# A written-out order of single operations, all stores by SyncE, a first chunk in halves and fewer warming products in a gated-linear-attention and mixture-of-attention kernel

## The chip, the cores and the metric

The kernel runs on one core of one Trainium2 chip. The metric is the device time of one execution in microseconds (us), as the median of several runs; smaller is better. Every time below is in us unless ns is written. The engines are PE (TensorE), DVE (VectorE), ACT (ScalarE), POOL (GpSimd) and SP (SyncE, which only issues transfers).

## The reference, cut to what matters

```python
for t in range(S):                       # B, H, S, D = 4, 8, 768, 48
    state = alpha[t, :, None] * state + outer(k[t], v[t])
    y[t] = q[t] @ state
x = y as (B, S, 384)
logits = x @ w_gate                      # 4 experts, the best 2 weighted by a softmax
for e in range(4):                       # Hd = 64
    q, k, v = x @ wq[e], x @ wk[e], x @ wv[e]
    a = softmax(causal(q @ k.T / 8))
    out += weight[e] * (a @ v @ wo[e])
```

## The kernel before, in words

**Stage one** turns the recurrence into 24 chunks of 128 tokens, six for each of the four batches. For chunk n, DVE makes the running products of alpha by two scans (L466 backwards, L489 forwards) and scales k (L493) and q (L497). PE then makes the products of k and q (`pa`, L527), transposes k (`pt`, L554), updates the state (`pu`, L572, for which ACT first copies the transposed k, `kt`), and makes the chunk's output (`py`, L618) from the masked products `ms`. The mask of one half is put on by DVE (L536), that of the other by an ACT copy (L539) and a POOL selection (L543).

**Stage two** works in eight units u of three chunks (384 tokens): projections of q and k (`pj`, L660; for unit 0 in plain fp32, L890, straight from the loaded weights `wqk`), values and gate (`pv`, L687; L679 for unit 0), scores (`sc`, L749), their masked copy with a running maximum on DVE (L758), the exponential on ACT (L767), the weighting on POOL (L786), transpositions (`tr`, L804) with a copy on ACT (L818), the product with the values (`yv`, L841), its split in two parts on ACT and DVE (L850, L852), and the output projection (`po`, L867), copied by ACT (L873) and stored. SP issues all loads and the stores (L879), save the last two stores, which ACT issues itself (L876).

**Form of a product.** PE uses its array in several forms: whole (`pj`, `pv`, `po`; transpositions `tr`, `pt`), in two bands of rows (`pa`, `sc`), in two bands of columns (`pu`, `yv`) or in four (`py`). All products write to eight PSUM banks `g`.

**What sets the order.** Every operation is recorded with the operations that it has to follow, its engine and the buffers that it uses. A planner with costs of its own for each operation then walks through them, and at each step takes, engine by engine, the ready operation of the lowest rank. The rank comes from `TURN`, a table of 552 numbers that orders groups of operations. Each engine's instructions are written down in the resulting order and run strictly in it. Before the first use of the last bank, the planner fills every gap that it expects on PE with products of zeros (`warm`, L1095), whose operand `zb` lies in the constant `d1r`.

**Verdict.** ACT squares and sums the running products of each chunk (L509). At the end a number made from these sums (`verdict`: two DVE instructions L514 and L515, a product on PE at L517, a DVE copy at L519) is read by every engine (L1104), which then branches round a slow exact version.

Of the kernel before, what the change touches and what calls it, by code (L numbers as in the profile page):

```python
# [49 lines left out]
STICK = 100  # L50
DMA_FIXED = 1.5
DMA_RATE = 250.0
LOOK = 0.05
WARM_GAP = 0.45
WARM_MM = 0.11
GB = 8
HINT = {"PE": 9.0, "V": 120.0, "A": 120.0, "G": 60.0, "S": 200.0}
TURN = (
# [24 lines left out]
)  # L83
# [1123 lines left out]
```

## Time and profile before

| | |
|---|---|
| time, median of 3 runs | 317.26 us (316.0 to 317.34) |
| profiled execution: own time, span of its instructions | 317.55 us, 315.8 us |
| PE, DVE, ACT, POOL busy in the span | 307.5, 243.9, 228.7, 119.1 us |
| products on PE, of these warming products | 3809, 56 |
| loaded, stored | 25.39 MB, 4.72 MB |

The own time is 1.75 us longer than the span, which runs from the first instruction to the last. A product in plain fp32 that isn't a transposition is recorded twice. Busy time of PE is the time in which any product is in flight: products overlap, so that the step from one start to the next tells more than the length of one.

### The profile page before, as it was taken

What the parts mean: (1) busy time and instruction counts of PE and PEld (TensorE: products, weight loads), DVE (VectorE), ACT (ScalarE), POOL (GpSimd) and SP (SyncE); (2) the same over time, 40 slices, a digit from 0 to 9 for tenths busy, and PEclk for the clock granted to TensorE, in tenths of its full rate; (3) what the DMA queues carried; (4) which work ended last, traced back from release to release, by engine and by line L of the source; (5) the groups of instructions that cost most, each with busy time, mean ns of one, the idle gap of its engine ahead of it and who ended that gap; (6) DMA issues with size and microseconds to landing.
All of it is one profiled execution on the core that took longest, in us unless ns stands there. A gap on an engine that the chain in (4) does not pass through costs nothing.

```text
span 315.8 us, 9736 instructions
## 1 busy us (share of the span) xinstructions
PE 307.5 (97%) x3809; PEld 270.4 (86%) x3809; DVE 243.9 (77%) x708; ACT 228.7 (72%) x591; POOL 119.1 (38%) x174
## 2 busy tenths in 40 slices
PE   8999999999999999999999999999999999999991
PEld 5899988999897998798999799899889978988791
DVE  6889999989899998898899999853883555376530
ACT  0885797576897799876696979965677886759661
POOL 5221464202651356561172646350507060507130
PEclk9999999999999999999999999999999999999998
DMA  7999933535513254331721440300101000012001
GB/s 205 296 241 228 234 124 124 169 88 155 153 26 117 72 155 124 103 103 55 220 98 28 115 134 16 112 4 1 52 27 51 28 2 1 2 50 75 27 29 56
DMA packets 14195, 30.79 MB, mean 97 GB/s; under 512 B 1664, under 2 KB 4960, under 8 KB 14144
## 3 DMA queue, kind: packets, MB, share of 16 engines
q1 hardware_dynamic: 13856, 29.72, 32.9%
q8 instruction: 31, 0.51, 0.7%
q10 hardware_dynamic: 288, 0.39, 0.3%
q14 instruction: 20, 0.16, 0.2%
HBM read 25.39 MB, written 4.72 MB: 95 GB/s over the span
## 4 chain that ended last, share of the span: by engine, by line
PE 94%; DVE 2%; ACT 1%; ACTq 1%; issue 1%; POOL 0%; POOLq 0%
PE g L660 14%; PE g L804 12%; PE g L841 12%; PE g L618 11%; PE g L749 10%; PE g L867 8%; PE g L527 7%; PE g L687 7%; PE g L572 3%; PE g L1095 3%; PE g L554 2%; PE g L890 2%; PE g L679 1%; ACTq L876 1%; DVE al L466 0%
## 5 line engine op out<-in xcount | busy, mean ns | idle before, releaser
L786 POOL TENSOR_SCALAR a<-a,cf,gw 128x128 f32<-128x128 f32 (+5 forms) x96 | 80.7, 854 | 77.0 <-DVE cf L779 19.6
L767 ACT ACTIVATE a<-a,mx 128x128 f32<-128x128 f32 (+5 forms) x96 | 63.3, 661 | 12.2 <-DVE mx L758 11.6
L758 DVE CUSTOM_DVE_ANT_0 a<-g,cm 128x384 f32<-128x384 f32 (+3 forms) x96 | 46.9, 529 | 9.6 <-PE g L749 9.4
L818 ACT ACTIVATE at<-g 128x512 f32<-128x512 f32 (+3 forms) x124 | 48.9, 465 | 1.2 <-PE g L804 0.6
L804 PE MATMUL g<-ident,a 128*128 128x128 f32 x336 | 46.1, 276 | 0.1
L804 PEld LDWEIGHTS g<-ident,a 128*128 128x128 f32 x336 | 37.9, 141 | 4.0 <-POOL a L786 1.2
L841 PE MATMUL g<-at,vg 128*64 128x384 f32 (+2 forms) x324 | 39.4, 391 | 0.0
L749 PE MATMUL g<-k,q 64*128 64x256 f32 (+3 forms) x384 | 37.6, 331 | 0.0
L841 PEld LDWEIGHTS g<-at,vg 128*64 128x64 f32 x324 | 21.7, 137 | 16.9 <-issue 13.6
L749 PEld LDWEIGHTS g<-k,q 64*128 64x128 f32 x384 | 29.8, 185 | 4.1 <-issue 0.6
L618 PE MATMUL g<-ms,vt 128*32 128x128 f32 x768 | 33.2, 275 | 0.0
L543 POOL TENSOR_SCALAR_AFFINE_SELECT ms<-ms 128x512 f32<-128x512 f32 x24 | 17.3, 722 | 41.8 <-ACT ms L539 41.7
L466 DVE TENSOR_TENSOR_SCAN al<-al,d1r 112x516 f32<-112x516 f32 (+1 forms) x25 | 30.5, 1226 | 1.6 <-POOL mask L432 1.6
L489 DVE TENSOR_TENSOR_SCAN al<-al,d1c 112x516 f32<-112x516 f32 (+1 forms) x25 | 30.5, 1223 | 0.2
L660 PE MATMUL g<-xh,wqk_h 128*128 128x384 f32 x84 | 29.8, 355 | 0.0
L660 PE MATMUL g<-xh,wqk_l 128*128 128x384 f32 x84 | 28.3, 337 | 0.0
L660 PE MATMUL g<-xl,wqk_h 128*128 128x384 f32 x84 | 28.2, 336 | 0.0
L509 ACT ACTIVATE al<-al 112x1033 f32<-112x1033 f32 x24 | 25.6, 1066 | 2.5 <-issue 1.6
L527 PE MATMUL g<-qk 48*128 48x128 f32 x384 | 26.1, 279 | 0.0
L527 PEld LDWEIGHTS g<-qk 48*128 48x128 f32 x384 | 23.2, 187 | 1.9 <-issue 0.6
L618 PE MATMUL g<-qk,S 112*32 112x128 f32 x480 | 24.2, 272 | 0.0
L589 POOL TENSOR_TENSOR C<-C,ev 112x192 f32<-112x192 f32 x16 | 10.4, 652 | 35.2 <-DVE C L587 30.6
(100 smaller groups left out, 642.3 us busy)
## 6 DMA issues: line engine op xcount, KB each, us to landing
qk<-in_qk_dram SPq DMA_DIRECT2D x24, 448.0 KB, 4.4
vt<-in_v_dram SPq DMA_DIRECT2D x25, 256.0 KB, 4.4
al<-in_al_dram SPq DMA_DIRECT2D x24, 226.2 KB, 4.1
out_dram<-ot SPq DMA_DIRECT2D x22, 192.0 KB, 1.9
at<-in_wqk_dram SPq DMA_DIRECT2D x1, 768.0 KB, 9.6
qk<-in_qk_dram SPq DMA_DIRECT2D x2, 224.0 KB, 3.4
at<-in_wvg_dram SPq DMA_DIRECT2D x1, 390.0 KB, 7.8
at<-in_wo_dram SPq DMA_DIRECT2D x1, 384.0 KB, 10.8
```

What stands on the lines that cost most here:

```text
L466: V.tensor_tensor_scan(backwards(al[0:P, AW + c0 - 1:AW + c1 - 1]), backwards(al[0:P, c0:c1]), d1r[0:P, sl].rearrange("p a w -> p (a w)"), ...
L489: V.tensor_tensor_scan(c, c, T(("d1c", n))[0:P, sl].rearrange("p a w -> p (a w)"), 0.0, OP.mult, OP.max)
L527: PE.matmul(T(("pa", n, s))[:, C * p:C * p + C], t[r:r + D, p, C:2 * C], t[r:r + D, p, 0:C], start=True, stop=True, tile_position=(r, 0))
L618: PE.matmul(py[32 * j:32 * j + 32, k], l, r, start=(i == 0), stop=(i == len(parts) - 1), tile_position=(0, 32 * j))
L660: PE.matmul(pj[:, :W3], w[:, kt, cs], x[:, kt, :], start=(i == 0), stop=(i == 8))
L749: PE.matmul(T(sk[e])[:, :w], q[r, x, ts], k[r, y, c0:c1], start=(m == 0), stop=(m == 2), tile_position=(64 * e, 0))
L758: V.tensor_tensor_reduce(T(ak[e])[:, c0:c1], T(sk[e])[:, :w], cm[:, m0:m0 + w], -1.0, mx[:, 0:1] if x else BIG, OP.add, OP.min, accum_out= ...
L767: A.activation(a[:, 0:n], a[:, 0:n], AF.Exp, bias=T(mk)[:, e, len(pieces) - 1:len(pieces)], scale=-1.0, accum_out=T(("sm", u))[:, ix:ix + 1])
L786: G.tensor_scalar(a[:, 0:n], a[:, 0:n], T(ck_)[:, e:e + 1], T(("gw", u))[:, i, eg:eg + 1], op0=OP.mult, op1=OP.mult)
L804: PE.transpose(pt[:, 128 * (j - j0):128 * (j - j0) + 128], a[:, 128 * j:128 * j + 128], ident)
L818: A.activation(dst, src, AF.Copy)
L841: PE.matmul(py[64 * e:64 * e + 64, lo:n1], v[:, j % 3, 64 * eg:64 * eg + 64], at[e][:, at_off(j) + lo:at_off(j) + n1], start=(j == 0), sto ...
```

## The change

1. `TURN` and the planner's choice among ready operations go. `ORDER` lists all 1573 operations one by one, and the planner only works out buffers and start times along it. Its costs are finer: a price for each pair of forms of a product, and slower products in the first 6 us.
2. Every store is issued by SP.
3. In chunk 0, `pt`, `pa`, the mask and `py` work on halves of two head pairs each, and DVE masks both parts.
4. A first exponential on a tile `junk` is added on ACT.
5. The warming products read a tile of their own (`zb` in an output buffer), and their number follows the new start times: 33 in place of 56.
6. Weights wait in planned `at` buffers, and not in fixed ones.

```diff
-TURN = (
-    215, 75, 5, 3, 42, 289, 74, 30, 19, 90, 221, 119, ...
+ORDER = (
+    15, 7, 0, 2, 4, 1, 3, 8, 6, 21, 31, 22, 24, 23, 13, 32, ...
...
-    def schedule(self, timed=True, turn=()):
+    def schedule(self, order=None):
...
+        for i in order:
             o = ops[i]
+            e = o["eng"]
+            assert (o["preds"] | o["claims"]) <= done
+            t = at[e]
+            for j in o["preds"]:
+                q = ops[j]
+                if q["eng"] != e or q["dma"]:
+                    t = max(t, q["end"] + SEM)
...
             if o["pe"]:
-                t = max(rt[i], t + change(o))
+                t = max(t, at["PE"] + turnover(state, o["pe"]))
+                state = o["pe"]
...
-                    warm(int(gap / WARM_MM * 0.8))
+                    cold = max(0.0, min(gap, COLD - pe))
+                    warm(int((cold / WARM_MM[0] + (gap - cold) / WARM_MM[1]) * 0.85))
...
-    zb = d1r.rearrange("p a b -> p (a b)").bitcast(BF)[:, 0:256]
+    zb = pools["ot"][1][:, 0:128].bitcast(BF)
...
+            op("G", 0.1, 0.15, lambda T: (G.memset(zb, 0.0), G.memset(junk, 0.0)) and None, w=whole(("junk",), ("zb",)), port=False)
+            op("A", 1.4, 1.5, lambda T: A.activation(junk, junk, AF.Exp), w=whole(("junk",)))
...
-                if s == 0 and n >= MS_ACT:
-                    op("V", 0.61, 0.69, f0, r=whole(("pa", n, s), ("mask",)), w=[(("ms", n), s)])
+                if n == 0 or (s == 0 and n >= MS_ACT):
+                    o, l = vec(np * C)
+                    op("V", o, l, f0, r=rd + whole(("mask",)), w=wr)
...
-            if u == NU - 1 and i:
-                op("A", 0.36, 0, lambda T: A.dma_start(out_d[b, t0:t0 + 128, :], T(("ot", u, i))),
-                   r=whole(("ot", u, i)), dma=196608)
-            else:
-                op("S", 0.06, 0, lambda T: SY.dma_start(out_d[b, t0:t0 + 128, :], T(("ot", u, i))),
-                   r=whole(("ot", u, i)), dma=196608)
+            op("S", 0.43, 0, lambda T: SY.dma_start(out_d[b, t0:t0 + 128, :], T(("ot", u, i))),
+               r=whole(("ot", u, i)), dma=196608)
...
                 for p in (0, 2):
                     prep_r(0, p, 2)
                     prep_c(0, p, 2)
+                    gla_t(0, p, 2)
+                    gla_a(0, p, 2)
```

DVE at the start of the program, before: chunk 0 (buffers `al_71`, `qk_75`) is prepared whole, then chunk 1's scans (`al_72`) follow, and the mask of chunk 0 (L536).

```order
L466 SCALAR_TENSOR_TENSOR al_71<-al_71,d1r 112x258 x2
L470 RECIPROCAL d1c_87<-al_71 112x2
L493 TENSOR_TENSOR qk_75<-qk_75,al_71 112x2x128
L470 RECIPROCAL d1c_87<-al_71 112x2
L489 SCALAR_TENSOR_TENSOR al_71<-al_71,d1c_87 112x258 x2
L497 TENSOR_TENSOR qk_75<-qk_75,al_71 112x2x128
L493 TENSOR_TENSOR qk_75<-qk_75,al_71 112x2x128
L497 TENSOR_TENSOR qk_75<-qk_75,al_71 112x2x128
L466 SCALAR_TENSOR_TENSOR al_72<-al_72,d1r 112x516
L470 RECIPROCAL d1c_87<-al_72 112x4
L489 SCALAR_TENSOR_TENSOR al_72<-al_72,d1c_87 112x516
L536 TENSOR_TENSOR ms_90<-g_64,mask 128x512
```

And now (the mask is L541 here):

```order
L493 TENSOR_TENSOR qk_75<-qk_75,al_71 112x2x128
L489 SCALAR_TENSOR_TENSOR al_71<-al_71,d1c_87 112x258
L470 RECIPROCAL d1c_87<-al_71 112x2
L493 TENSOR_TENSOR qk_75<-qk_75,al_71 112x2x128
L497 TENSOR_TENSOR qk_75<-qk_75,al_71 112x2x128
L466 SCALAR_TENSOR_TENSOR al_72<-al_72,d1r 112x516
L541 TENSOR_TENSOR ms_90<-g_64,mask 128x256
L489 SCALAR_TENSOR_TENSOR al_71<-al_71,d1c_87 112x258
L541 TENSOR_TENSOR ms_90<-g_63,mask 128x256
L497 TENSOR_TENSOR qk_75<-qk_75,al_71 112x2x128
L470 RECIPROCAL d1c_87<-al_72 112x4
L493 TENSOR_TENSOR qk_76<-qk_76,al_72 112x4x128
```

The first half's q is ready before the second half's forward scan, its mask comes between, and chunk 1's scan now stands ahead of the second half's.

PE about an eighth into the program, before: the output of one chunk (L618) stands alone between a transposition (L804) and scores (L749).

```order
L804 MATMUL g_66<-ident,a_129 128x128
L618 MATMUL g_67<-ms_91,vt_82 32x128 x4
L618 MATMUL g_67<-qk_78,S_94 32x128 x4
L618 MATMUL g_67<-ms_91,vt_82 32x128 x4
L618 MATMUL g_67<-qk_78,S_94 32x128 x4
L618 MATMUL g_67<-ms_91,vt_82 32x128 x8
L618 MATMUL g_67<-qk_78,S_94 32x128 x4
L749 MATMUL g_64<-k_104,q_101 128x256
```

And now, at the same chunk (number 3, buffers `ms_91` and `vt_79`), where the output products are at L628 and the state's at L582:

```order
L628 MATMUL g_69<-ms_90,vt_81 32x128 x8
L628 MATMUL g_69<-qk_77,S_95 32x128 x4
L628 MATMUL g_64<-ms_91,vt_79 32x128 x4
L628 MATMUL g_64<-qk_75,S_94 32x128 x4
L628 MATMUL g_64<-ms_91,vt_79 32x128 x4
L628 MATMUL g_64<-qk_75,S_94 32x128 x4
L628 MATMUL g_64<-ms_91,vt_79 32x128 x8
L628 MATMUL g_64<-qk_75,S_94 32x128 x4
L582 MATMUL g_68<-vt_79,kt_89 64x48
```

The outputs of chunks 2 and 3 are neighbours, so that PE enters and leaves their form once for the two.

ACT at the end of the program, before: the last two output copies (L873), each followed by its store.

```order
L850 ACTIVATE yh_141<-g_64 128x128
L850 ACTIVATE yh_141<-g_65 128x128
L873 ACTIVATE ot_144<-g_66 128x384
L876 DMA out_dram<-ot_144 128x384
L873 ACTIVATE ot_145<-g_70 128x384
L876 DMA out_dram<-ot_145 128x384
L1104 TENSOR_LOAD cnt
```

And now (copies at L889; the stores stand on SP, behind the earlier ones):

```order
L866 ACTIVATE yh_141<-g_64 128x128
L509 ACTIVATE al_74,acc<-al_74 112x1033
L866 ACTIVATE yh_141<-g_69 128x128
L889 ACTIVATE ot_145<-g_67 128x384
L889 ACTIVATE ot_144<-g_63 128x384
L1118 TENSOR_LOAD cnt
```

No store stands between the two copies, and the last chunk's square (L509) has moved here, between the two splits.

## Rows read from the trace of the kernel before

**Rows 1.** The page: busy time by engine, and the chain that ended last by engine.

```profile
PE 307.5 (97%) x3809; PEld 270.4 (86%) x3809; DVE 243.9 (77%) x708; ACT 228.7 (72%) x591; POOL 119.1 (38%) x174
...
PE 94%; DVE 2%; ACT 1%; ACTq 1%; issue 1%; POOL 0%; POOLq 0%
```

**Rows 2.** Changes of form: PE timeline (start, us, engine, line, operation), two places.

```profile
172.31 0.44 PE L660 MATMUL g<-xh,wqk_h 128*128 128x384 f32 x1
172.59 0.34 PE L660 MATMUL g<-xl,wqk_h 128*128 128x384 f32 x1
172.76 0.33 PE L660 MATMUL g<-xh,wqk_l 128*128 128x384 f32 x1
...
247.35 0.34 PE L867 MATMUL g<-wo_h,yl 128*128 128x384 f32 x1
247.62 0.44 PE L749 MATMUL g<-k,q 64*128 64x384 f32 x2
```

**Rows 3.** The end: timeline of PE, ACT and SP (q: the sequencer issues).

```profile
303.71 0.33 SPq L879 DMA_DIRECT2D out_dram<-ot  x1
...
307.16 0.28 ACT L850 ACTIVATE yh<-g 128x128 fp32r<-128x128 f32 x1 [1.01 <-PE g L841]
308.98 2.97 ACTq L876 DMA_DIRECT2D out_dram<-ot  x1
...
309.08 0.34 PE L867 MATMUL g<-wo_h,yl 128*128 128x384 f32 x1
...
312.05 0.49 ACT L873 ACTIVATE ot<-g 128x384 f32<-128x384 f32 x1 [3.10 <-issue]
312.57 0.34 ACTq L876 DMA_DIRECT2D out_dram<-ot  x1
```

**Rows 4.** The page, groups: squares on ACT, and issues with median us to landing.

```profile
L509 ACT ACTIVATE al<-al 112x1033 f32<-112x1033 f32 x24 | 25.6, 1066 | 2.5 <-issue 1.6
...
out_dram<-ot SPq DMA_DIRECT2D x22, 192.0 KB, 1.9
...
at<-in_wqk_dram SPq DMA_DIRECT2D x1, 768.0 KB, 9.6
```

**Rows 5.** The start: timeline of PE and of SP's issue of `wqk`.

```profile
1.55 7.63 PE L1095 MATMUL g<-d1r 128*128 128x256 bf16 x44 [1.55 <-POOL d1r L427]
...
5.02 0.51 SPq L395 DMA_DIRECT2D at<-in_wqk_dram  x1
...
12.70 1.08 PE L618 MATMUL g<-ms,vt 128*32 128x128 f32 x32
13.71 0.60 PE L554 MATMUL g<-ident,qk 112*128 112x112 f32 x4
14.25 1.16 PE L527 MATMUL g<-qk 48*128 48x128 f32 x16
```

**Rows 6.** The start: DVE timeline (in brackets idle time before, and what ended it).

```profile
10.76 0.69 DVE L536 TENSOR_TENSOR ms<-g,mask 128x512 f32<-128x512 f32 x1 [0.66 <-PE g L527]
11.92 0.36 DVE L584 TENSOR_TENSOR C<-g,ev 112x192 f32<-112x192 f32 x1 [0.47 <-PE g L572]
...
12.79 0.68 DVE L497 TENSOR_TENSOR qk<-qk,al 112x512 f32<-112x512 f32 x1
```

**Rows 7.** Busy by window: PE, weight loads, DVE, ACT, POOL; granted clock; DMA.

```profile
20.00:120.00 100.00, 99.93 (x1445) 89.74 (x1444) 94.77 (x252) 74.99 (x196) 38.02 (x54) 1.00 0.51 142
2.00:6.00 4.00, 4.00 (x20) 2.82 (x19) 2.89 (x7) 0.00 (x0) 2.93 (x12) 1.00 0.99 283
7.00:8.80 1.80, 1.80 (x19) 1.58 (x18) 1.76 (x4) 1.30 (x2) 0.13 (x1) 1.00 1.00 261
```

**Rows 8.** The verdict's product, PE timeline.

```profile
211.39 0.19 PE L517 MATMUL g<-ones,okm 112*1 112x1 f32 x2 [0.29 <-ACT at L818]
```

**Rows 9.** Waits of SP's queue: us in total, times, longest.

```profile
SPq L879 <- ACT ot L873: 72.2, 17, 19.2
```

More of the change, by code (lines that the diff above doesn't have):

```diff
@@ L144, in op @@
         return i
-    def schedule(self, timed=True, turn=()):
+    def schedule(self, order=None):
         ops, pools = self.ops, self.pools
-        place = {g: x for x, g in enumerate(turn)}
-        rank = [0] * len(ops)
-        for x, o in enumerate(sorted(ops, key=lambda o: (place.get(o["grp"], o["grp"]), o["i"]))):
-            rank[o["i"]] = x
-        slot_of, done = {}, [None] * len(ops)
+        order = list(order or range(len(ops)))
+        slot_of = {}
         free = {p: [(0.0, x) for x in range(len(t))] for p, t in pools.items()}
@@ L155, in schedule @@
         last = {}
-        queue = {p: [] for p in pools}
-        need = []
         seen = set()
         for o in ops:
-            new = [k for k in o["keys"] if k not in seen and k[0] in self.kinds]
-            seen.update(new)
-            o["new"] = new
-            for k in new:
-                queue[self.kinds[k[0]]].append(k)
-        strict = {p for p in pools if p != "g"}
-        succ = [[] for _ in ops]
-        miss = []
-        for o in ops:
-            miss.append(len(o["preds"]) + len(o["claims"]))
-            for j in o["preds"] | o["claims"]:
-                succ[j].append(o["i"])
-        ready = {e: [] for e in ("PE", "V", "A", "G", "S")}
-        rt = [0.0] * len(ops)
-        for o in ops:
-            if not miss[o["i"]]:
-                ready[o["eng"]].append(o["i"])
-        at = {e: ISSUE for e in ready}
-        pos = {p: 0 for p in pools}
-        dma_at = port_at = 0.0
-        order = []
-        state = ["pj"]
-        def change(o):
-            a, b = state[0], o["pe"]
-            if MODE.get(a) == MODE.get(b):
-                return 0.0
-            return LEAVE.get(a, 0.096) + ENTER.get(b, 0.105)
-        def est(i):
-            o = ops[i]
-            t = max(rt[i], at[o["eng"]])
+            o["new"] = [k for k in o["keys"] if k not in seen and k[0] in self.kinds]
+            seen.update(o["new"])
+        at = {e: ISSUE for e in ("PE", "V", "A", "G", "S")}
+        dma_at = port_at = 0.0
+        state = "pj"
+        done = set()
+        for i in order:
+            o = ops[i]
+            e = o["eng"]
[5 more added lines that the diff above has]
+                    t = max(t, q["end"] + SEM)
+                elif e != "PE":
+                    t = max(t, q["end"] + SAME)
+            for j in o["claims"]:
+                t = max(t, ops[j]["start"])
             if o["port"]:
@@ L194, in est @@
             if o["pe"]:
-                t = max(rt[i], t + change(o))
-            cnt = {}
+                t = max(t, at["PE"] + turnover(state, o["pe"]))
+                state = o["pe"]
             for k in o["new"]:
-                p = self.kinds[k[0]]
-                c = cnt.get(p, 0)
-                if p in strict and (pos[p] + c >= len(queue[p]) or queue[p][pos[p] + c] != k):
-                    return None
-                if c >= len(free[p]):
-                    return None
-                t = max(t, sorted(free[p])[c][0])
-                cnt[p] = c + 1
@@ L248, in schedule @@
             o["end"] = end
-            order.append(i)
+            done.add(i)
             for k in o["keys"]:
@@ L528, in f @@
                                   start=True, stop=True, tile_position=(r, 0))
[L529 to L530 removed]
+            op("PE", 0.225 * np, 0.225 * np + 0.27, f, pe="pa", r=[(("qk", n), (x, p)) for x in "kq" for p in ps_] + whole(("zb",)),
+               w=[(("pa", n, s), p) for s in (0, 1) for p in ps_], use=[("ms", n)])
             for s in (0, 1):
+                rd, wr = [(("pa", n, s), p) for p in ps_], [(("ms", n), (s, p)) for p in ps_]
@@ L605, in f @@
                 L = None if first else T(("S", n))
-                for k in range(3):
+                for k in ks:
                     if k < 2:
@@ L619, in f @@
                                       tile_position=(0, 32 * j))
-            occ = (8 if first else 14) * 0.111
-            r = [(("qk", n), ("q", p)) for p in range(4)] + whole(("vt", n), ("ms", n))
-            if not first:
-                r += whole(("S", n))
-            op("PE", occ, occ + 0.17, f, r=r, pe="py",
-               w=whole(("py", n)), use=[("at", -3)] if plain and u == 0 else [("xh", u), ("xl", u)])
+            use = [("at", -3)] if plain and u == 0 else [("xh", u), ("xl", u)]
+            if n == 0:
+                for ks, ps_ in (((0,), (0, 1)), ((1, 2), (2, 3))):
+                    op("PE", 0.222 * (2 * len(ks) - 1), 0.222 * (2 * len(ks) - 1) + 0.17, lambda T, ks=ks: f(T, ks), pe="py",
+                       r=[(("qk", n), ("q", p)) for p in ps_] + whole(("vt", n)) + [(("ms", n), (s, p)) for s in (0, 1) for p in ps_],
+                       w=[(("py", n), ks[0])], use=use)
+            else:
+                occ = (8 if first else 14) * 0.111
+                r = [(("qk", n), ("q", p)) for p in range(4)] + whole(("vt", n), ("ms", n))
+                if not first:
+                    r += whole(("S", n))
+                op("PE", occ, occ + 0.17, f, r=r, pe="py", w=whole(("py", n)), use=use)
             def fh(T):
```

163 lines of the change are left out of this document (67 added, 96 removed), and 97 rows, old and new, of tables (ORDER, TURN).

## The prediction

> **What bounds the kernel now.** I read the page first. PE is in flight for 307.5 of 315.8 us, and the chain that ended last runs on PE for 94% [rows 1]. So the kernel is one stream of products, and its time is (work of the products) + (steps lost between forms) + (PE waiting or warming) + (what follows the last product). The last product starts at 309.08 [rows 3]. From 13.71 on [rows 5] I compared the step from each start to the next with the usual step of its kind: PE hardly ever waits there; 1.8 us in all is unexplained, the verdict's product among it. From 20 to 120 us it is in flight for 99.93 of 100 us [rows 7]. Before 13.71 it has done only one chunk's `pt`, `pa`, `pu` and `py`, some 3.1 us of steps, so that 10.6 us of the start are waiting or warming. A gain has to come out of one of these places; faster work on ACT or POOL is worth nothing by itself. DVE is the second to watch: 94.77 busy in 20 to 120 us [rows 7].
>
> **Steps between forms.** Of products of 384 columns that follow each other in one form, the step is 0.17 (172.59 to 172.76) [rows 2]. The first one after the column form of `pu` takes 0.28 to the next (172.31 to 172.59), and the last one ahead of scores 0.27 (247.35 to 247.62): entering or leaving costs 0.1. Projections and transpositions both use the whole array, and a change between those two adds only 0.01 in the median over all such starts. I counted the changes in the two orders. Before, 195 (warming products aside): 101 dear ones, 69 between full forms, 25 between two kinds that share their bands. Now 156: 83, 45 and 28. For each kind of change I took, over all starts of the trace, the median step across it less the usual step: the dear ones come to 14.9 us, 0.148 each, all 195 to 16.4. At the same prices (three changes that the trace hasn't, at 0.13) the 156 come to 13.2. **Term: -3.2.** The bounds are 18 dear changes at one side each, 18 x 0.09 = 1.6, and at both sides, 18 x 0.20 with 0.5 for the others = 4.1. The products themselves stay the same in number and shape, save the split of chunk 0. Of the shown place, the two outputs side by side save one entry and one exit.
>
> **The end.** After the last product ACT ought to copy at once, but its copy starts at 312.05, idle for 3.10 before: the store that ACT issued itself at 308.98 held it for 2.97 [rows 3]. The next issue on ACT took 0.34, and SP's at 303.71 took 0.33 [rows 3]. With all stores on SP the copy can begin some 0.1 after the last product's end, at 309.5 instead of 312.05; the store's issue follows as before, and its way to landing is no longer (median 1.9 on SP) [rows 4]. What is moved here: the two stores come to SP's queue 1.05 apart, behind no load, since SP has none left there. The last square (L509, 1.07 each) [rows 4] now stands on ACT between the last two splits; before, ACT was idle for 1.01 ahead of the second one (307.16) [rows 3], so that this split comes 0.1 late at most, and what it splits is read only by the last six products. The verdict goes behind the last product: a product, a DVE copy and the read of `cnt` on five engines, about 1.5 us in a row, beside a landing that takes 1.9 and its closing waits. If that cover were gone, it would cost the 0.5 by which the chain might outlast the landing. **Term: -2.5**, bounds 0 (SP's issue is held for 2.97 as ACT's was) and -2.7.
> The Trainium skill says in "Trainium Kernel Development and Optimization", section Key Constraints, that transfers issued from SP, ACT and POOL run on the same 16 engines, and that issuing from several of them saves only the sequencer's issue time. By it two issues on one queue would be worth 0.3 us the other way, the sum 3 us less; the row with 2.97 on ACT against 0.33 on SP is what I go by, and it is larger than such an issue.
>
> **The start.** PE's second chunk begins at 14.25 with `pa` [rows 5], right behind q of chunk 1, which DVE ends at 12.79 + 0.68 = 13.47 [rows 6]. On DVE's way there 0.66 + 0.47 = 1.1 was waiting for products of chunk 0 [rows 6]. In the new order the mask of the first half stands behind a scan of 1.2, and its products are ready by then, so these waits go. Two half masks are added ahead (0.8), and one whole mask (0.69) goes behind: q of chunk 1 ends at 13.47 - 1.1 + 0.8 - 0.7 = 12.5, and `pa` could start 1.7 earlier (14.25 to 12.5). But three quarters of chunk 0's `py` (0.8 of the 1.08 at 12.70) then come behind it: 0.9 is left. The next gate is the load of `wqk`: issued at 5.02 and landed 9.6 later, at 14.6 [rows 4, 5]. It was the last of 2,988 KB, and is now the last of 3,080: at some 245 KB a us, 15.0. In the new order PE comes to the first projection behind this `pa` (1.1, estimated as twice the 0.54 from 13.71 to 14.25), the 0.8 of `py` and one `pu` (0.3): at 12.5 + 2.2 = 14.7, so it waits 0.3 there, and 0.6 is left. Then DVE decides: more of its work is ahead of the points where PE needs it (chunks 2 and 3 prepared together). It has 5.2 us to spare from 20 to 120 us and is asked for the same work about 2 us sooner, so it fits, narrowly. **Term: -0.6**, bounds -0.9 (all of it stays) and 0 (DVE gives none).
> Fewer warming products (22 in place of 44 in the first row) cost nothing if the first real one comes early enough. The early exponential is not early: in ACT's order it stands at row 198, and the one table load stands ahead of the first copy either way. It is worth nothing, and costs one tiny instruction (under 0.3, ACT is 75% busy there).
>
> **The verdict's wait.** In the middle, PE waited 0.29 for its sums [rows 8], with 0.1 for its forms: **-0.4**, with the bounds of all other waits, -1.8 (none is left) and +2 (the new order brings some of its own).
>
> **The sum.** -3.2 - 2.5 - 0.6 - 0.4 = -6.7. The profiled execution took 317.55, 0.3 over the median; 317.55 - 6.7 = 310.85, and 0.3 less for a median: **310.6**.
>
> **The rivals.**
> *DVE becomes the bound in the first third.* For: 94.8% busy, and idle time on an in-order engine can't all be used. Against: what it waits for comes from PE, which then lags. If DVE gives back the start and a third of the steps' gain with 1 us of waits: 310.6 + 0.6 + 1.1 + 1 = 313.3.
> *SP's store holds like ACT's.* The 2.97 is that queue's first store; SP's queue has issued about a hundred transfers by then, and its 303.71 is a store, which speaks against. Term of the end 0: 313.1.
> *The clock.* In 2 to 6 us some 19 warming products start in 4 us, steps of 0.21; from 7.0 to 8.8 about 17 in 1.8, steps of 0.11 [rows 5, 7]: the level of 1.2 GHz, then that of 2.4, after products without a break since 1.55, though the granted clock reads 1.00 in both. With half the products and gaps between, the step up could come later. Real work between 7 and 16 us is some 6 us of steps; if half of it that is on the path ran at the lower level: +2.5, 313.1. Against: the 22 products still last 4.7, and real ones follow.
> The Trainium skill ("TensorE: Matmul & The Clock Gate", Part 1) has it that the clock starts at half and that activity releases it, idle time takes it back; by that rule it would be this rival.
> *Slower: loads behind stores on SP.* SP's queue is strict, and its stores waited 72.2 us in all for ACT's copies, the longest 19.2 [rows 9]. A load of alpha or qk behind such a store, needed less than that later, makes DVE wait and PE after it. From 8.3 us of such waits on PE the gain is gone (317.26 + 1.6 needs 8.3 over 310.6); at 10 us it gives 320.6. For: five of the first stores stand between loads in the new order. Against: SP's 22 stores did no harm before [rows 4], with buffers for four chunks ahead.
>
> **Chances.** Forecast 0.66 (308.5 to 312.5); DVE 0.17; SP's store 0.05; the clock 0.05; loads behind stores 0.04; no effect at all, since what PE gains is lost to waits of many kinds, 0.03 (316 to 318). A measurement of this kernel tells about 0.5%, 1.6 us (its runs lie within 1.4). Faster takes the first four, and a part of the others: 0.92; same 0.04; slower 0.04. The range reaches from the lower end, where all terms lie at their good bounds but one (310.6 - 2.1), to beyond the three rivals: 308.5 to 313.9.
>
> **What would show it.** The ends: the last copy on ACT with no idle time from an issue, and the span's end some 3.8 after it starts. The steps: PE's last product about 303.9 to 305.5 into the span. The start: `pa` of chunk 1 at 12.5, the first fp32 projection at 15. DVE: over 96% busy from 5 to 60 us. Wrong would be: idle rows on PE released by DVE or transfers of more than 3 us in all, steps of 0.21 after 8 us, or a 3 us issue on SP at the end.

## The result and the profile after

The changed kernel takes 319.41 us in the median of 20 runs (317.38 to 322.5), the kernel before 316.76 (315.8 to 317.75). The ratio is 1.0081 (95% interval 1.0068 to 1.0095): it is slower by 2.6 us, where I had forecast 310.6. The profiled execution took 318.9, its span is 317.07, 1.25 longer than before. This pair shows about half of the difference, since the profiled execution of before (317.55) lies above its median and that of after below.

The page, busy time and chain by engine:

```profile
PE 304.1 (96%) x3786; PEld 271.7 (86%) x3786; DVE 246.6 (78%) x711; ACT 227.4 (72%) x592; POOL 120.2 (38%) x175
...
PE 83%; DVE 4%; DMA 4%; ACT 3%; SPq 1%; POOL 1%; issue 1%; POOLq 0%; DVEq 0%; ACTq 0%
```

PE was 94% of the chain before [rows 1]. Now DVE, ACT and a transfer stand in it: PE waits for them.

The end, timelines of PE and ACT:

```profile
309.32 0.33 PE L883 MATMUL g<-wo_h,yl 128*128 128x384 f32 x1
309.59 0.19 PE L517 MATMUL g<-ones,okm 112*1 112x1 f32 x2
...
309.74 0.49 ACT L889 ACTIVATE ot<-g 128x384 f32<-128x384 f32 x1 [0.59 <-PE g L883]
```

PE's last output product starts at 309.32 (309.08 before [rows 3]), nothing saved. ACT's copy follows it at once, 2.3 earlier than the one at 312.05 in [rows 3]. And yet the span ends 1.25 later. What lies there is seen in the branch behind the read of the verdict (all instructions of its line: engine, operation, duration, first and last start) and in SP's waits:

```profile
L1119 SPq EVENT_SEMAPHORE  x8: 17/17/17, 315.2 to 315.7; - x8
L1119 ACTq COMPARE_BRANCH  x1: 68/68/68, 310.6 to 310.6; - x1
L1119 POOLq COMPARE_BRANCH  x1: 65/65/65, 310.7 to 310.7; - x1
...
L1119 ACTq EVENT_SEMAPHORE  x1: 17/17/17, 311.1 to 311.1; - x1
L1119 SPq COMPARE_BRANCH  x1: 70/70/70, 311.2 to 311.2; - x1
...
L1119 DVEq EVENT_SEMAPHORE  x1: 21/21/21, 311.3 to 311.3; - x1
L1119 POOLq EVENT_SEMAPHORE  x1: 17/17/17, 314.9 to 314.9; - x1
...
SPq L1119 <- SPq L1119: 3.9, 1, 3.9
```

The branch itself takes 0.07. ACT and DVE go on about 0.5 later, but POOL only at 314.9 and SP at 315.2, 4.2 and 3.9 after their branches, waiting for nothing else that the profile shows. The last store had landed by then (issued at about 310.3; with the median way of 1.9 that is 312.2). In the same 5 us two instruction queues move seven packets (transfers from 311 to 316):

```profile
q14 instruction: 6, 0.05, 3.0%
q8 instruction: 1, 0.02, 1.6%
```

Five of the seven start between 311.75 and 312.16, about 1 us behind the five branches, and the last of these is through at 313.2. In t2 and t4 (below), where ACT and SP branch last, two packets follow, again 1.0 to 1.7 us behind. I read the wait of POOL and SP as a wait for code. It is a reading and not shown: ACT, DVE and PE go on before the first packet, POOL and SP 1.7 and 1.9 us behind the end of the fifth, and no run left the branch out. The Trainium skill has such a wait in "Runtime: NRT & Kernel Launch", section Instruction fetch mechanics: a taken branch whose target isn't in the two pages at hand forces a fetch of the page before the engine goes on. The packets fit that; the page gives no price, and here it is 4 us. I had not drawn on it.

For the rest I compared, as in the prediction, every step on PE with the usual step of its kind, and added up what is over: PE's waits. What remains up to the last product is its work, changes of form included. (Parts are rounded, so that sums and differences can be 0.1 off.)

| us | before | changed | forecast | measured |
|---|---|---|---|---|
| PE's work (changes of form) | 296.9 | 293.2 | -3.2 | -3.6 |
| waits and warming up to 20 | 10.6 | 12.0 | -0.6 | +1.4 |
| waits after 20 | 1.6 | 4.1 | -0.4 | +2.5 |
| start of the last product to the end of the span | 6.7 | 7.7 | -2.5 | +1.0 |
| span | 315.8 | 317.1 | -6.7 | +1.25 |

Where the start goes (DVE, then PE), and the largest of the later waits (PE, DVE):

```profile
11.80 0.69 DVE L493 TENSOR_TENSOR qk<-qk,al 112x512 f32<-112x512 f32 x1 [1.51 <-DMA qk<-in_qk_dram]
12.42 1.22 DVE L489 TENSOR_TENSOR_SCAN al<-al,d1c 112x516 f32<-112x516 f32 x1
...
13.81 0.68 DVE L497 TENSOR_TENSOR qk<-qk,al 112x512 f32<-112x512 f32 x1
...
17.60 1.58 PE L902 MATMUL g<-at,at 128*128 128x128 f32 x12 [0.51 <-DMA at<-in_wqk_dram]
...
99.79 1.42 PE L820 MATMUL g<-ident,a 128*128 128x128 f32 x11 [1.25 <-DVE q L688]
...
94.98 1.89 DVE L489 TENSOR_TENSOR_SCAN al<-al,d1c 112x516 f32<-112x516 f32 x1
...
99.06 0.21 DVE L730 TENSOR_REDUCE gt<-gt 128x12 f32<-128x48 f32 x1
99.18 0.55 DVE L688 TENSOR_TENSOR q<-g,q 128x384 fp32r<-128x384 f32 x1
```

q of chunk 1 ends at 13.81 + 0.68 = 14.49, not at the 12.5 of my sum and later than before (13.47 [rows 6]): the product with k waits for its load, and the scan behind it, whose data is there, waits with it. Behind that the first fp32 projection (L902) starts at 17.60, when `wqk` has landed (17.46; 14.65 before). At 97 PE stands for 1.4 (1.25 in this row) until DVE has split q and freed a bank.

### The profile page after: what moved, and what is told of

It reads as the page before. It is cut to its first block, busy times and chain, and to the rows that moved or that the text cites. A ratio compares the mean times of both kernels' runs of the same rounds, so it can differ in the third digit from the quotient of the medians.

```text
span 317.1 us, 9640 instructions
## 1 busy us (share of the span) xinstructions
PE 304.1 (96%) x3786; PEld 271.7 (86%) x3786; DVE 246.6 (78%) x711; ACT 227.4 (72%) x592; POOL 120.2 (38%) x175
## 4 chain that ended last, share of the span: by engine, by line
PE 83%; DVE 4%; DMA 4%; ACT 3%; SPq 1%; POOL 1%; issue 1%; POOLq 0%; DVEq 0%; ACTq 0%
PE g L820 11%; PE g L676 11%; PE g L628 11%; PE g L857 10%; PE g L765 10%; PE g L883 8%; PE g L703 7%; PE g L530 7%; DMA at<-in_wqk_dram 4%; PE g L582 3%; PE g L902 3%; PE g L563 2%; ACT a L783 2%; PE g L695 1%; POOL a L802 1%; DVE a L774 1%
## 5 line engine op out<-in xcount | busy, mean ns | idle before, releaser
L802 POOL TENSOR_SCALAR a<-a,cf,gw 128x256 f32<-128x256 f32 (+5 forms) x96 | 80.3, 847 | 84.8 <-DVE cf L796 51.6
L783 ACT ACTIVATE a<-a,mx 128x128 f32<-128x128 f32 (+5 forms) x96 | 63.5, 663 | 13.5 <-DVE mx L774 12.3
L834 ACT ACTIVATE at<-g 128x512 f32<-128x512 f32 (+3 forms) x124 | 50.0, 462 | 12.7 <-PE g L820 12.3
L774 DVE CUSTOM_DVE_ANT_0 a<-g,cm 128x512 f32<-128x512 f32 (+3 forms) x96 | 47.9, 528 | 7.6 <-PE g L765 5.0
L820 PE MATMUL g<-ident,a 128*128 128x128 f32 x336 | 44.2, 275 | 1.7 <-DVE q L688 1.3
L549 POOL TENSOR_SCALAR_AFFINE_SELECT ms<-ms 128x512 f32<-128x512 f32 x23 | 16.2, 711 | 59.6 <-ACT ms L545 59.4
L857 PEld LDWEIGHTS g<-at,vg 128*64 128x64 f32 x324 | 24.4, 137 | 13.1 <-issue 7.9
L765 PEld LDWEIGHTS g<-k,q 64*128 64x128 f32 x384 | 30.7, 185 | 3.8 <-issue 0.9
L628 PE MATMUL g<-ms,vt 128*32 128x128 f32 x768 | 32.8, 274 | 0.0
L676 PE MATMUL g<-xh,wqk_h 128*128 128x384 f32 x84 | 29.0, 345 | 0.0
L509 ACT ACTIVATE al<-al 112x1033 f32<-112x1033 f32 x24 | 25.6, 1068 | 1.6 <-DVE qk L497 0.9
L530 PEld LDWEIGHTS g<-qk 48*128 48x128 f32 x384 | 24.0, 190 | 2.3 <-DVE qk L497 0.9
L628 PE MATMUL g<-qk,S 112*32 112x128 f32 x480 | 24.2, 272 | 0.0
L628 PEld LDWEIGHTS g<-ms,vt 128*32 128x32 f32 x768 | 20.9, 109 | 2.2 <-issue 0.3
```

Source lines behind the costliest of these rows:

```text
L530: PE.matmul(T(("pa", n, s))[:, C * p:C * p + C], t[r:r + D, p, C:2 * C], t[r:r + D, p, 0:C], start=True, stop=True, tile_position=(r, 0))
L628: PE.matmul(py[32 * j:32 * j + 32, k], l, r, start=(i == 0), stop=(i == len(parts) - 1), tile_position=(0, 32 * j))
L676: PE.matmul(pj[:, :W3], w[:, kt, cs], x[:, kt, :], start=(i == 0), stop=(i == 8))
L765: PE.matmul(T(sk[e])[:, :w], q[r, x, ts], k[r, y, c0:c1], start=(m == 0), stop=(m == 2), tile_position=(64 * e, 0))
L774: V.tensor_tensor_reduce(T(ak[e])[:, c0:c1], T(sk[e])[:, :w], cm[:, m0:m0 + w], -1.0, mx[:, 0:1] if x else BIG, OP.add, OP.min, accum_out= ...
L783: A.activation(a[:, 0:n], a[:, 0:n], AF.Exp, bias=T(mk)[:, e, len(pieces) - 1:len(pieces)], scale=-1.0, accum_out=T(("sm", u))[:, ix:ix + 1])
```

## The experiments

All runs in one table: the median, the ratio to the kernel before on the same chip, and the four parts of the span as above. The parts belong to one execution each.

| run | median | ratio (95%) | waits to 20 | after 20 | work | end |
|---|---|---|---|---|---|---|
| before, second profile (x0) | 317.5 | one run | 11.2 | 1.2 | 296.8 | 6.5 |
| changed, again (y4) | 319.2 | 1.0102 (1.0078 to 1.0126) | 11.1 | 4.2 | 293.2 | 7.3 |
| t1, hint later | 320.85 | 1.0126 (1.0093 to 1.0158) | 11.7 | 5.3 | 293.2 | 7.5 |
| t2, verdict early | 320.09 | 1.0102 (1.0077 to 1.0127) | 11.6 | 6.6 | 293.5 | 6.3 |
| t3, t2 and stores on ACT | 317.68 | 1.0029 (1.0011 to 1.0048) | 11.2 | 6.0 | 293.5 | 5.1 |
| t4, before with stores on SP | 316.51 | 0.9992 (0.9982 to 1.0002) | 10.2 | 1.7 | 296.9 | 6.4 |
| w1, splits ahead of gates | 318.52 | 1.0070 (1.0043 to 1.0098) | 11.2 | 4.3 | 293.2 | 7.5 |
| w2, scan behind masks | 318.97 | 1.0090 (1.0062 to 1.0119) | 10.7 | 5.0 | 293.2 | 7.3 |
| x2, both, further | 318.65 | 1.0064 (1.0039 to 1.0089) | 11.1 | 4.3 | 293.2 | 7.6 |
| z1, a scan left out | 319.08 | 1.0047 (1.0012 to 1.0083) | 13.2 | 3.1 | 293.2 | 7.7 |
| w3, scan ahead of k | 318.98 | 1.0130 (1.0073 to 1.0187) | 11.0 | 5.1 | 293.2 | 7.5 |
| w4, w3 and wqk earlier | 318.89 | 1.0060 (1.0039 to 1.0080) | 12.1 | 4.3 | 293.2 | 7.5 |
| x1, more warming | 320.04 | 1.0076 (1.0039 to 1.0113) | 11.6 | 6.7 | 293.2 | 7.7 |
| z2, half of wqk | 318.51 | 1.0060 (1.0029 to 1.0091) | 11.7 | 4.2 | 293.2 | 7.5 |
| y2, 22 changes of form more | 325.69 | 1.0287 (1.0265 to 1.0309) | 12.9 | 7.0 | 296.6 | 7.4 |
| y3, no early exponential | 318.87 | 1.0064 (1.0042 to 1.0087) | 11.7 | 5.2 | 293.2 | 7.3 |
| x3, all mends | 317.12 | 0.9996 (0.9979 to 1.0014) | 11.3 | 4.4 | 293.5 | 4.9 |
| y1, x3 with wo's split later | 317.53 | 1.0013 (0.9991 to 1.0036) | 13.8 | 4.2 | 293.5 | 5.1 |

The order of the changed kernel spreads over 3 to 5 us from run to run, mostly in its first 40 us. Differences of one microsecond between two of these medians are therefore not taken as shown; the parts of a profile are.

### The end

```diff
-HINT = {"PE": 9.0, "V": 120.0, "A": 120.0, "G": 60.0, "S": 200.0}
+HINT = {"PE": 9.0, "V": 120.0, "A": 120.0, "G": 20.0, "S": 20.0}
```

> The changed kernel, with the mark that tells SP and POOL ahead of the branch which way it goes put nearer to the end (20 us by the plan, in place of 200 and 60). In the changed kernel SP and POOL stand still for 3.9 and 4.2 us between the branch and the next instruction, DVE, ACT and PE for 0.5. Theory A: the code behind the branch is no longer at hand on SP and POOL; then both resume under 0.8 after the branch, the end follows the last store's landing (312.1) by 1.4, the span falls from 317.1 to 313.5 and the time by 3.6. Theory B: five engines load code at once and the last two wait for the others; then the 4 us stay and the time is that of the changed kernel.

The branch in this run:

```profile
L1119 POOLq COMPARE_BRANCH  x1: 65/65/65, 311.5 to 311.5; - x1
...
L1119 SPq COMPARE_BRANCH  x1: 70/70/70, 312.1 to 312.1; - x1
L1119 POOLq EVENT_SEMAPHORE  x1: 17/17/17, 314.8 to 314.8; - x1
...
SPq L1119 <- SPq L1119: 3.7, 1, 3.7
```

POOL stands for 3.2, SP for 3.7: the place of the hint cures nothing. Either theory A is wrong or the mark doesn't bring the code; no run separates these two. The next one separates an engine's own wait from engines in each other's way.

Verdict early: the square of chunk 20 and the four instructions of the verdict are moved in `ORDER`, ACT's square to about 240 us, the product to about 277.

> The changed kernel, with chunk 20's square and the verdict moved back to about 40 us before the end, all stores still on SP. POOL, DVE, PE and ACT then branch early or one after the other, SP still behind its last store. Theory A (SP's own code load, 3.9 us, begins when SP branches): SP resumes about 4 us after its branch at 311.2, so that the span stays within 1 of 317.1. Theory B (engines in each other's way): SP resumes in under 1 us and the span falls by 3.5, to 313.5. A third, that the late verdict as such costs the time (a product, two DVE operations, a read), gives 1.5 back.

```profile
L1119 POOLq COMPARE_BRANCH  x1: 65/65/65, 304.6 to 304.6; - x1
...
SPq L1119 <- SPq L1119: 2.5, 1, 2.5
```

POOL now branches 6 us earlier and is hidden. SP, last at the end, still stands for 2.5, and the end takes 6.3 in place of 7.7 or 7.3. So most of SP's wait is its own (theory A); 0.9 to 1.4 of it is there only when five engines branch at once (theory B). The time shows no gain, since PE waits 2.4 more after 20 us than in the second profile of the changed kernel. Of this 0.6 is the earlier square's, at 243 us, where two squares stand on ACT ahead of the copy of the state (L604) that PE needs (PE):

```profile
244.01 0.43 PE L628 MATMUL g<-qk,S 112*32 112x128 f32 x8 [0.43 <-ACT S L604]
```

The rest lies elsewhere, some 0.8 of it at 28 us, where the square is not.

The same with this edit in `outp`:

```diff
+            if u == NU - 1 and i:
+                op("A", 0.36, 0, lambda T: A.dma_start(out_d[b, t0:t0 + 128, :], T(("ot", u, i))),
+                   r=whole(("ot", u, i)), dma=196608)
+            else:
```

> The changed kernel with the end of the one before: verdict early, last two stores on ACT. Theory A: SP's branch comes 5 us before the end and its load is hidden; ACT is held for 3 us by its first store as before (2.97), the second copy starts at about 312.3, the span ends 3.75 after it, 316.0. If ACT isn't held (the hold came from something else than a first issue on that queue), the copy starts at 309.7 and the span ends at 313.5.

The end falls to 5.1, the time to 317.68. SP has branched at 307.5, 8 us ahead of the end. ACT is not held: its first store took 0.39 here, where I had expected 2.97. Whether that row of before was an accident, the kernel before tells itself:

> The kernel before, unchanged, profiled a second time. My term for the end rested on one row, ACT's store issue that held it for 2.97 us. If that hold belongs to the kernel (theory A), it is there again, between 2.7 and 3.2, and the span is 315 to 316. If it comes and goes (theory B, since the same issue took 0.39 on ACT in the run with the verdict early), it is under 0.6 here and the last store lands about 2.5 earlier after the last product.

```profile
309.14 2.77 ACTq L876 DMA_DIRECT2D out_dram<-ot  x1
312.01 0.49 ACT L873 ACTIVATE ot<-g 128x384 f32<-128x384 f32 x1 [2.90 <-issue]
```

It is there again (theory A). It belongs to that kernel and not to a first store on ACT as such, since in t3, x3 and y1 (the last two below) the first store on ACT takes 0.39. Why, no run shows.

The one edit alone, on the kernel before:

> The kernel before with one edit, its last two stores on SP. Theory A: the last copy starts at 309.5 in place of 312.05, SP branches at about 311.0 and resumes at 315.0; the span is 316.3, 0.5 longer than before, so that the edit is worth nothing or less. Theory B: SP resumes at once, the span is 313.3, 2.5 shorter.

```profile
309.17 0.49 ACT L873 ACTIVATE ot<-g 128x384 f32<-128x384 f32 x1 [0.55 <-PE g L867]
...
SPq L1101 <- SPq L1101: 2.5, 1, 2.5
```

The copy comes at once, as my prediction had it, and SP's branch, now behind the last store, gives nearly all of it back: the end is 6.4 against 6.7 and 6.5, the time 0.9992 (0.9982 to 1.0002). The term that I put at -2.5 is worth -0.3 at most; the interval includes nothing.

### The waits after 20 us

DVE's order at 97 us:

```diff
+L688 TENSOR_TENSOR q_102<-g_67,q_102 128x384
+L688 TENSOR_TENSOR k_104<-g_70,k_104 128x384
 L724 TENSOR_REDUCE gm_110<-vg_108 128x3
...
-L688 TENSOR_TENSOR q_102<-g_67,q_102 128x384
```

> The changed kernel with two DVE splits of unit 2 (L688) put ahead of the seven small gate operations of that unit (L724 to L730). At 97 to 99.8 us of the changed kernel PE waits 1.4 us for a bank that the first of these splits frees, and this split stands behind 1.9 us of gate work. Theory (the new order gives back its gain to waits at single places like this one): the wait goes, PE's last product and the time come 1.2 to 1.4 us earlier. Rival (DVE as a whole is the bound there, 97% busy): the work ahead of the next need is the same, PE waits a little later for as long, the time stays within 0.4.

PE's wait fell only from 1.4 to 1.07, and what ended it was another: ACT's copy of transposed weights, behind the gate's exponential, which now came later. The rival is nearer than the theory. The same at 137 us:

> The changed kernel with one DVE scan (L466, chunk 19) put behind the masks of chunks 12 and 13 (L541). In three of the four profiles of this order the scan waits at 137 us for its load, issued only when ACT's square of chunk 14 frees the buffer, and the mask that PE waits for stands behind it; PE loses 0.14 to 1.08 us there. Theory: the wait at 137 falls under 0.1 in the profile, and the time by some 0.6. Rival (what is lost there is lost at another place when it isn't lost there): no change.

The wait in run t1 that this was aimed at (DVE, PE), and in w2 (PE):

```profile
137.00 1.23 DVE L466 TENSOR_TENSOR_SCAN al<-al,d1r 112x516 f32<-112x516 f32 x1 [0.41 <-DMA al<-in_al_dram]
138.15 0.67 DVE L541 TENSOR_TENSOR ms<-g,mask 128x512 f32<-128x512 f32 x1
...
138.87 1.48 PE L765 MATMUL g<-k,q 64*128 64x384 f32 x12 [0.50 <-DVE ms L541]
```

```profile
139.80 0.43 PE L628 MATMUL g<-ms,vt 128*32 128x128 f32 x8 [0.53 <-DVE mx L774]
```

The mask comes in time, the scan now delays the next masked copy (L774), and PE waits 0.73 in all for that. In the third run of this kind the gate's exponential on ACT is put behind three copies too, and the scan moved to where DVE has room:

> The changed kernel with the two DVE splits ahead of the gate operations as before, the gate's exponential on ACT put behind three copies that PE waits for (where the wait had moved to), and the scan of chunk 19 put 75 places further back, where DVE has room (79% busy from 140 to 160 us). Theory (waits at single places, each mended by its order): the waits at 97 and 137 both fall under 0.2, the time is 1.6 to 2.1 lower, 317.5. Rival (DVE is the bound from 60 to 140 us, whatever the order): the loss from 90 to 140 us stays above 1.2 and the time above 318.4.

At 137 nothing is left (0.1 between 100 and 140). At 97 the wait stays at 1.07, now for POOL's weighting (L802), whose factors come from DVE. The time, 318.65, is nearer to the rival's. So DVE, ACT and POOL ended this wait one after the other, as the order was mended. I took each to be late because DVE is, and tested that without touching the order:

```diff
-                V.tensor_tensor_scan(c, c, T(("d1c", n))[0:P, sl].rearrange("p a w -> p (a w)"), 0.0, OP.mult, OP.max)
+                return V.tensor_tensor_scan(c, c, T(("d1c", n))[0:P, sl].rearrange("p a w -> p (a w)"), 0.0, OP.mult, OP.max) if n != 10 else None
```

> The changed kernel without the forward scan of chunk 10 on DVE (L489, 1.89 us at 95 us; chunk 10's output is left wrong by it), nothing else. Three mends of the order at 97 us took only 0.35 of PE's wait of 1.4 there. Theory (DVE's load: between 20 and 100 us it is busy for 97% and the new order asks for more of it sooner): with 1.9 us of DVE work less the wait at 97 falls under 0.4 and what PE has lost by 140 us falls by 1 or more, the time by about 1. Rival (POOL's weighting or ACT's copies set that wait by themselves): it stays above 1.

```profile
97.91 4.54 PE L820 MATMUL g<-ident,a 128*128 128x128 f32 x37
```

The transpositions are now one row, with no idle time in it; the wait, by the steps, is 0.26. PE loses 1.1 from 90 to 140 us, against 1.6 in the first profile and 2.1 in the second of the changed kernel; it would be less if this execution didn't lose 0.6 more at 137 than the first. DVE's work made the wait at 97. Whether it is all the work that DVE has from 20 to 100 us, or the one scan close ahead of the split, this run doesn't tell apart. (The profiled execution, which is also the median one, took no less time because it lost 13.2 in the start.)

### The start

DVE's order, chunk 1:

```diff
 L470 RECIPROCAL d1c_87<-al_72 112x4
+L489 SCALAR_TENSOR_TENSOR al_72<-al_72,d1c_87 112x516
 L493 TENSOR_TENSOR qk_76<-qk_76,al_72 112x4x128
-L489 SCALAR_TENSOR_TENSOR al_72<-al_72,d1c_87 112x516
```

> The changed kernel with the forward scan of chunk 1 (L489) put back ahead of the product with k (L493), as in the kernel before; warming products as many as in the changed kernel. In the changed kernel L493 waits 1.51 for the load of qk, and the scan, whose data is there, stands behind it, so that q of chunk 1 ends at 14.49 and not at 13.47. Theory (this order costs the start 1 us): q ends at 13.3. Rival (wqk's landing, at 17.5, is the next gate): PE then waits that much longer for the first projection, and nothing of it is left at 20 us. I expect the rival to be right by more than half: time lower by 0 to 0.5.

q of chunk 1 ends at 13.04, as the theory has it, and then PE stands for the load of `wqk`, which landed at 16.28:

```profile
12.36 0.68 DVE L497 TENSOR_TENSOR qk<-qk,al 112x512 f32<-112x512 f32 x1
...
16.41 1.57 PE L902 MATMUL g<-at,at 128*128 128x128 f32 x12 [0.77 <-DMA at<-in_wqk_dram]
```

That is the rival's mechanism. The loss up to 20 is 11.0, within what the same order shows without the edit (10.7 to 11.7 in the other profiles of the changed order whose start reads a clock of 1.00 throughout). I can't call it a gain. And with `wqk` ahead of v of chunk 1 and alpha of chunks 2 and 3 in SP's order:

> The same, and the load of wqk put ahead of v of chunk 1 and alpha of chunks 2 and 3 (708 KB): it lands at about 14.5 instead of 17.5. If both gates together make the late start, what PE has lost by 20 us falls from 12.0 to about 10.8 and the time by 1.2; if v of chunk 1 or alpha then come too late, the loss only moves to 18 to 40 us.

`wqk` landed at 13.2, and alpha now comes too late. DVE and PE:

```profile
16.20 2.36 DVE L466 TENSOR_TENSOR_SCAN al<-al,d1r 112x516 f32<-112x516 f32 x2 [3.18 <-DMA al<-in_al_dram]
...
19.19 0.42 PE L628 MATMUL g<-ms,vt 128*32 128x128 f32 x8 [2.34 <-DVE ms L541]
```

The loss stays at 12.1: what one load gains another loses. Warming products, 5 to 14 and 6 to 10 at two places, 13 more in all (the first number in the expectation counts weight loads with them):

> The changed kernel with 26 more warming products... in rows, 13 more pairs of weights and product: 14 in place of 5 ahead of the state of chunk 0 and 10 in place of 6 ahead of the second half's pa; no other edit. In the profile of the changed kernel PE idles for 1.3 us at 9 us and the granted clock is 0.5 from 10.1 to 13.5. Theory (fewer warming products cost the clock, and the clock costs time): no stretch at 0.5 before 20 us, time lower by 0.3 to 0.8. Rival (the real products there wait for loads anyway): time within 0.3 of the changed kernel's 319.4.

The clock stayed at 1.00, as expected, and the time did not fall. PE instead waited for another load (DVE, PE):

```profile
29.59 0.96 DVE L421 TENSOR_TENSOR wo_l<-at,wo_h 128x768 fp32r<-128x768 f32 x1 [0.88 <-ACT wo_h L406]
...
29.88 0.94 PE L530 MATMUL g<-qk 48*128 48x128 f32 x12 [0.83 <-ACT vg L712]
```

ACT stood before its split of `wo`, issued at 18.56 and landed at 28.7 here, and the copy that PE needed stood behind it. Before, `wo` was issued at 5.6; it now waits for an `at` buffer. So that split was moved back:

> The best kernel so far (waits at 97 and 137 mended, verdict 38 us before the end, last two stores on ACT; warming as in the changed kernel), and with it the split of wo (L406 on ACT, L421 on DVE) behind some 20 further operations of ACT. wo is first multiplied at about 75 us, but in five of nine profiles of this order ACT stands before its split for the load, which was issued 12 us later than in the kernel before, and PE loses 0.3 to 1.1 at 27 to 29 us. Theory (loads that come later in the new order make the start long and uneven): the loss from 20 to 40 us falls under 0.5, the time to 316.5 or less. Rival (another load takes its place): 317.1 as before.

From 20 to 40 us PE lost under 0.1, as the theory has it. But this execution had lost 13.8 by 20, with the granted clock at 0.5 from 13.6 to 20.4, and at 45 us PE lost 0.7 more than in the changed kernel, behind the moved split's part on DVE (L421, at 42.7). The time is that of x3. Last, with half of `wqk` loaded:

> The changed kernel with half of wqk loaded (384 KB in place of 768 KB; the other half is set to zero on POOL at the start, so the projections of unit 0 and later ones use wrong weights), nothing else. Theory (the start up to 40 us is paced by the order and bytes of the loads): wqk lands 1.5 earlier and so does what follows it; what PE has lost by 40 us falls from 12.3 in the mean of twelve profiles to 11 or less, and the time by 1 or more. Rival (DVE's order paces the start): the loss by 40 us stays above 11.8.

`wqk` landed at 15.0, in place of 17.5 in the first profile (15.4 to 17.3 in the others with all of it), and PE waited for no load, but the loss by 40 was 11.8. It is undecided, because the clock stood at 0.5 here too, just under the first real products (window, PE busy and so on; the clock is the 1.00 or 0.50; then this run's and the changed kernel's chunk 0 outputs):

```profile
14.20:17.40 3.20, 3.20 (x47) 2.44 (x44) 2.71 (x4) 2.68 (x6) 1.01 (x2) 0.50 1.02 251
```

```profile
14.63 1.51 PE L632 MATMUL g<-ms,vt 128*32 128x128 f32 x24
```

```profile
10.10:13.50 3.40, 3.34 (x30) 2.60 (x30) 1.89 (x4) 0.00 (x0) 0.18 (x1) 0.50 1.06 300
...
15.63 0.86 PE L628 MATMUL g<-ms,vt 128*32 128x128 f32 x24
```

24 products last 1.51 at 0.50 and 0.86 at 1.00.

### Changes of form, and the exponential

Eleven pairs of neighbours on PE exchanged in `ORDER`, such as `tr`, `tr`, `sc`, `sc` to `tr`, `sc`, `tr`, `sc`:

> The changed kernel with eleven pairs of neighbours on PE exchanged from 160 us on, so that 22 dear changes of form are added and no work. Theory of the prediction (a dear change costs 0.148 on PE's path): PE's last product comes 22 x 0.148 = 3.3 later, the time 2.6 to 3.6 higher than the changed kernel's on this chip. Rival (it is hidden in waits for other engines, and the 3.2 forecast for 39 changes fewer was never there): under 1.

PE's work rose from 293.2 to 296.6: 3.4 for 22 changes, 0.156 each. The profile's span is 8.1 longer than in the second profile of the changed kernel (the medians differ by 6.5), and the rest of it is waits, 4.6 more. Of these 1.8 lie in the first 20 us, which the edit doesn't touch, and nearly all others from 187 to 246 us, where pairs were exchanged: an order moved in eleven places cost nearly as much in waits (2.8) as in changes.

> The changed kernel without the added exponential. I forecast nothing for it, since it stands at place 198 of ACT and the table is loaded ahead of the first copy either way: same table load at 0.81, time within 0.5 of the changed kernel's. Rival: without it a table load appears ahead of the first exponential at 29 us, 1.3 longer there.

One table load at the same place, and a time within the spread: the exponential is worth nothing.

> The changed kernel itself, unchanged, as the measure for the other three on this chip, and a second profile of it. If its losses are those of the order, the waits at 97 (1.4) and the resumption of SP 3.7 to 4 after its branch are there again; if the start is uneven, what PE has lost by 40 us differs from 12.3 by over 0.3.

Its own second profile has the wait at 97 (1.40) again, and SP's, at 3.4 a little under what was expected; the loss by 40 us is 11.1, against 12.3. So the waits at 97 and of SP come with the order, and the start is uneven.

### All mends together

> All that helped or may help in one kernel: the order of the last, the added warming products, the verdict about 38 us before the end (its last square in an idle stretch of ACT), and the last two stores on ACT. Losses that go by the profiles so far: waits 1.9, the end 2.6 (7.74 from the last product's start to the end in the changed kernel, 5.13 with the verdict early), the clock 0.3. 319.4 - 4.8 = 314.6, which would be 2 us under the kernel before. Rival: waits move elsewhere, 316.5 or more.

```profile
309.07 0.39 ACTq L892 DMA_DIRECT2D out_dram<-ot  x1
309.58 0.49 ACT L889 ACTIVATE ot<-g 128x384 f32<-128x384 f32 x1 [0.54 <-PE g L883]
```

The end is 4.9, the profile's span 314.1, and the median 317.12: the kernel before, and no better (0.9996, 0.9979 to 1.0014). The mends take back what the change cost, most of it at the end, but the 314.6 of the expectation doesn't come: the start (11.3) and the waits after 20 (4.4) are as long as before the mends. In eleven runs its mean granted clock is never under 0.996; y1, with the fewer warming products, goes down to 0.985.

## Why the prediction was wrong

**Steps between forms: right.** -3.2 forecast, -3.6 measured in both profiles of either kernel, and 0.156 for a change by y2. The price was read where PE hardly waits, and it held. The sum was 8.0 off in this pair: 3.5 by the end, 2.9 by the waits and 2.0 by the start, less 0.4 here.

**The end: the step that failed first.** I wrote that the verdict behind the last product takes "about 1.5 us in a row beside a landing that takes 1.9", and 0.5 if the cover were gone. I priced the read and put what follows it at nothing: SP and POOL go on only 2.9 to 4.2 us after the branch in every profile where five engines branch together. In the kernel before, POOL branches at 302 and SP at 304.7, so that [rows 3], which I read to the last store, could not show it. The place of ACT's 2.97 is taken by SP's 2.5 (t4), by 3.9 with all engines at once. +1.0 in place of -2.5. The rival "SP's store holds like ACT's" gave the time of that case by another mechanism.

**The start.** "Its products are ready by then, so these waits go" holds, but DVE has another gate, the load of qk at 11.8 (the same load lands at 11.6 before), ahead of which the new order puts nothing that could run: the scan stands behind. And `wqk` landed at 17.46, not at 15.0 (15.4 to 17.3 in the other profiles of this order). I took one rate for bytes in order, where several loads share the transfers: when it landed, 4.1 MB had been moved, some 0.9 MB of them not among my 3,080 KB (0.6 MB beside the 2,988 KB before), and in the first 14.65 us the mean rate was 228 GB/s, against 251 before. w3 shows that this load is the next gate: with q earlier, PE stood for `wqk`. +1.4 in this pair; over all profiles of the changed order with the start unedited, 10.7 to 13.8 against 10.2 to 11.2 in three of before.

**The waits: the forecast had the wrong sign.** I gave -0.4 with a bound of +2; it was +2.5. DVE as a bound was my first rival, with 1 us of waits in the first third. It came true at 97 us (1.4), and z1 shows DVE's work as the cause there. The 5.2 us that DVE had "to spare" from 20 to 120 were not where they were needed. At 137 (0.14 to 1.08) DVE stands ahead of PE too, but it waits for a load itself. What lies beyond these two, at 216, 237, 263 and 287 (1.3 in all), was not tried, and its cause stays open.

**The clock rival** happened: a granted clock of 0.5 of the 2.4 GHz, the level of 1.2, from 10.1 to 13.5, behind a stretch in which PE waited for a load (busy 0.36 of the 1.6 us from 8.5 to 10.1). "TensorE: Matmul & The Clock Gate" of the Trainium skill, Part 1, would have had this step down from idle time; the row agrees. In the median it is small: of 19 runs (without the one of 322.5) the six with a mean clock under 0.99 took 319.5, the others 319.2. Where the stretch is longer it isn't. Two profiles whose starts have the same order, and where `wqk` landed at 16.1 in both, show it: w2 with a clock of 1.00, and z1 with 0.50 from 13.1 to 19.9 (first w2, then z1):

```profile
16.21 1.58 PE L902 MATMUL g<-at,at 128*128 128x128 f32 x12 [0.77 <-DMA at<-in_wqk_dram]
```

```profile
13.10:19.80 6.70, 6.47 (x65) 5.71 (x66) 5.51 (x10) 4.84 (x9) 1.58 (x3) 0.50 1.02 262
...
17.79 2.59 PE L902 MATMUL g<-at,at 128*128 128x128 f32 x12
```

PE comes 1.6 later to its first projection, no longer waits for the load, and takes 1.0 more for it: 2.5 more are lost by 20 us (13.2 against 10.7). (PE was 0.4 late in z1 before the clock fell, at `pa` of chunk 1; w2's wait of 0.77 would have covered that.) The one other profile with so long a stretch, y1, lost 13.8. The four with one half as long lost 11.2 to 12.9, the six without one 10.7 to 11.7.

**Loads behind stores** was not the case: the late loads at 137 were behind ACT's square of an older chunk (SP's wait for L509), not behind a store.

What stays open is the rest of the spread of the first 40 us. Loads (x1, w4) and the clock (z1, y1) both show in it; z2, which was to separate them, had the low clock too.

## What to carry to other kernels

Price the end of a kernel by the last instruction of every engine, also of those that do no work: here a branch that was hidden in mid-stream cost 2.5 to 4 us behind the last store. A stream that is busy for 97% has no room that an average shows: of the work taken out of it (3.6 us, as forecast) nothing was left here, since waits after 20 us gave 2.5 back and the start 1.4, and the largest of these waits was for the second engine, at 94% with its own order. And where moving one instruction only uncovers the next wait, take work away instead, to see which engine it is.

## What the runs showed of the hardware

After the branch at the end SP stood for 3.4 to 3.9 us where five engines branched together, and for 2.5 to 2.7 where it did not (t2, t3, t4, x3, y1 and the kernel before). POOL stood for 2.9 to 4.2 in the first case, for 2.5 to 2.8 in t2, t3, x3 and y1, and for 1.3 in the kernel before and in t4. ACT, DVE and PE went on 0.4 to 1.1 us after theirs. Instruction packets moved in the same time; a hint placed 20 us ahead of the end didn't change it (3.2 and 3.7). ACT's first store held ACT for 2.77 and 2.97 in the two profiles of the kernel before and for 0.39 in three kernels with another order. Neither was looked for. A granted clock of 0.5 for 6.8 us under the first real products cost 2.5 us (z1 against w2).
